# A fused causal convolution and gated MLP on one core: the first unit's convolution moved to channel-major taps, and the weights' first load cut in two

## The chip, the cores and the metric

The kernel runs on one core of a Trainium2 chip. Its time is the device time of one execution in microseconds (us). The core has a matrix engine (TensorE, PE in the profile, whose weight loads are shown as PEld), a vector engine (VectorE, DVE), a scalar engine with activation tables (ScalarE, ACT), a general engine (GpSimd, POOL) and a sync engine that only issues transfers and waits (SyncE, SP). "Line 552" or "L552" is a line of the kernel before.

## The reference

The input is `x` of shape 8 x 4096 x 192. Each of 8 heads (24 channels each) has 7 taps. The taps go through a softmax and then weight the last 7 positions, causally within each of the 8 sequences. The result, 32768 tokens of 192 channels, goes through a two-layer network with the activation h * cos(h):

```python
w = np.exp(weight - np.max(weight, axis=-1, keepdims=True))
w = w / (np.sum(w, axis=-1, keepdims=True) + 1e-09)          # 8 heads x 7 taps
out = np.einsum('hk,bskhg->bshg', w, x_unf)                   # causal, 7 taps
h = x @ w_in            # 192 -> 2048
g = h * np.cos(h)
return g @ w_out        # 2048 -> 192
```

## The kernel before, in words

**Tiling.** Tokens are worked on in 32 units of 1024, each of two tiles of 512 tokens, so there are 64 tiles. For a tile, the first product (`mm1`, L503) makes `h` in 8 pieces h0 to h7 of 256 hidden channels each: six matmuls per piece, in pairs that use the upper and the lower 64 rows of the array, into one buffer of a ring of three in PSUM (`h_pool`). ACT makes the cosine (`s0` to `s7`, L510), DVE multiplies (`g`, L514). The second product (`mm2_step`, L552) sums over the 16 blocks of hidden channels into two further PSUM banks (`o_pools`), in 64 steps of two matmuls per tile. Its results are copied to SBUF and stored.

**Convolution.** `mm1` wants the convolved tokens channel-major (`cT`). Units 4 to 31 use a path that the change does not touch. Units 1 to 3 cast x to bf16 on POOL (`cast_unit`, L219), multiply by a banded 128 x 128 matrix per head (`band`, L229), copy the token-major result to `ct`, double it and transpose it by a DMA. Unit 0 is the start of the kernel, and its path is written out by hand:

1. One small matmul (L150) spreads the 8 x 7 weights over the partitions. DVE and ACT do the softmax there (L176 to L185).
2. DVE multiplies a mask by the taps (`prod`, L401), sums over the taps (`diag`, L404), and 16 small copies spread the sums into `band`: seven on DVE, seven on POOL, two on ACT (L415).
3. The first half of x (4 blocks of 128 tokens) is cast on ACT (L219). 32 matmuls with `band` convolve it (`conv_first`, L432). The results are doubled on the way out (L438), turned by 12 matmuls against the identity (`turn_first`, L453) and copied into `cT` (L457).
4. The second half of unit 0 is loaded later, convolved behind h3 (`conv_rest`, code `r`, L465 and L472) and turned by a DMA transpose (code `X0`, L326).

**Order.** Nothing is scheduled automatically: each engine runs its instructions in the order in which the program writes them. For each tile a string gives PE's order and one gives ACT's. In these strings `h0` to `h7` are pieces of `mm1` (`h0a`, `h0b` are halves in tokens), `m11` is 11 steps of `mm2`, `w5` is five matmuls on zeros that only keep PE running (`keep_warm`, L136), `W0` and `W1` cast the two halves of `w_out` on POOL (L120), `K1` casts unit 1's x on POOL, `d11`, `c11` are the two halves of unit 1's banded convolution, `ed11`, `ed21`, `ec11`, `ec21` their copies on ACT, `D1` and `X1` its doubling and its transpose, `L2` loads unit 2. The ACT strings also set DVE's order, since each `s` is followed by its multiplication. For the first tile:

```python
PE_FIRST[0] = "K1 h0a h0b W0 h1 h2 h3 r h4 w5 d11 w4 h5 d21 W1 c11 X0 m1 h6 m11 h7 L2 c21 D1"
ACT_FIRST[0] = "s0a s0b s1 s2 er s3 s4 ed11 ed21 s5 ec11 s6 ec21 s7"
```

**Transfers.** `w_in` comes as two transfers on POOL's queue (`load_w`, L112), cast on the way. x and `w_out` come on SP's queue, in order. Two waits are put into that queue by hand: the second half of unit 0 and unit 1 wait for `diag`; `w_out` (L124) waits for the second copy of `conv_first`.

Of the kernel before, what the change touches and what calls it, by code (L numbers as in the profile page):

```python
# [16 lines left out]
def kernel(  # L17
# [14 lines left out]
    T = 512  # L32
# [25 lines left out]

    xf = x.rearrange("b s d -> (b s) d")
# [20 lines left out]
    w_row = consts.tile([4, HQ * K], FP32)  # L80
    nc.scalar.dma_start(out=w_row, in_=weight.rearrange("(q h) k -> q (h k)", q=4))
# [26 lines left out]
    w_src = moe_w_in.rearrange("(m k) (t f) -> t m k f", k=NC, t=2)  # L108
# [18 lines left out]

    one = consts.tile([128, 1], FP32)
    nc.vector.memset(one, 1.0)
    zero = consts.tile([128, T], BF16)  # L130
    nc.vector.memset(zero, 0.0)  # L131
    idle = o_pools[0].tile([128, T], FP32, name="o_ps0")

    def keep_warm(n, bank=idle):
        for _ in range(n):
# [3 lines left out]
    quarter = consts.tile([4, 128], FP32)  # L139
    nc.gpsimd.memset(quarter, 1.0)  # L140
    nc.gpsimd.affine_select(out=quarter, in_=quarter, compare_op=ALU.is_ge, fill=0.0, base=0, pattern=[[1, 128]],
                            channel_multiplier=-32)
    nc.gpsimd.affine_select(out=quarter, in_=quarter, compare_op=ALU.is_ge, fill=0.0, base=31, pattern=[[-1, 128]],
                            channel_multiplier=32)
# [4 lines left out]
    w_bc = w_all[:, 0 : HQ * K].rearrange("p (h k) -> p h k", k=K)  # L149
# [4 lines left out]
    xb0 = consts.tile([128, UB + 1, D], BF16, name="x_bf0")  # L154

    E = 32 + K - 1
    mask = consts.tile([128, E, K], BF16)
    nc.gpsimd.memset(mask[0:32], 0.0)
    nc.gpsimd.affine_select(out=mask[0:32], in_=mask[0:32], compare_op=ALU.not_equal, fill=1.0, base=1 - K,  # L159
                            pattern=[[1, E], [1, K]], channel_multiplier=-1)  # L160
    band = consts.tile([128, H, 256], BF16)
    nc.vector.memset(band, 0.0)
    for q, copy in enumerate((nc.vector.tensor_copy, nc.scalar.copy, nc.scalar.copy)):
        copy(out=mask[32 * q + 32 : 32 * q + 64], in_=mask[0:32])  # L164
    for t in range(2):
        load_w(t)
    nc.gpsimd.memset(xb0[:, 0, :], 0.0)
    ident = consts.tile([128, 128], BF16)
    nc.gpsimd.memset(ident, 0.0)
    nc.gpsimd.affine_select(out=ident, in_=ident, compare_op=ALU.not_equal, fill=1.0, base=0, pattern=[[1, 128]],  # L170
                            channel_multiplier=-1)
    wn = consts.tile([128, HQ, K], BF16)
    ct_bufs = [consts.tile([128, 2 * NC * NPB + 1, 64], BF16, name="ct_buf%d" % i) for i in range(2)]

    wmax = consts.tile([128, HQ, 1], FP32)
    nc.vector.tensor_reduce(out=wmax[:, :, 0], in_=w_bc, axis=mybir.AxisListType.X, op=ALU.max)  # L176
    wexp = consts.tile([128, HQ, K], FP32)
    nc.vector.tensor_tensor(out=wexp, in0=w_bc, in1=wmax.to_broadcast([128, HQ, K]), op=ALU.subtract)
    nc.scalar.activation(out=wexp, in_=wexp, func=AF.Exp)
    nc.scalar.activation(out=scrap, in_=one, func=AF.Sin)  # L180
    wsum = consts.tile([128, HQ, 1], FP32)
    nc.vector.tensor_reduce(out=wsum[:, :, 0], in_=wexp, axis=mybir.AxisListType.X, op=ALU.add)
    winv = consts.tile([128, HQ, 1], FP32)
    nc.vector.reciprocal(winv, wsum)
    nc.vector.tensor_tensor(out=wn, in0=wexp, in1=winv.to_broadcast([128, HQ, K]), op=ALU.mult)  # L185
    wo = consts.tile([128, NP, 2, D], BF16)

# [19 lines left out]
    def cast_unit(u, n0=0, n1=UB + 1, copy=nc.gpsimd.tensor_copy):  # L207
# [8 lines left out]
        if n0 == 0:  # L216
            bf[u] = xb0 if u == 0 else xbf_pool.tile([128, UB + 1, D], BF16, name="x_bf")
        o = 1 if u == 0 else 0
        copy(out=bf[u][:, n0 + o : n1 + o, :].rearrange("p n (h k r) -> p (n h) k r", k=NC, r=R),  # L219
# [3 lines left out]
    have = {("whole", 0, 0)}  # L223
# [24 lines left out]
    def conv_part(u, c, banks, whole=False):  # L248
# [6 lines left out]
        if u == 1 and c == 0:  # L255
            spread_taps(ps[1][:, nb * 2 * G : nb * 2 * G + K])
# [4 lines left out]
        for b in range(2):  # L261
            conv_out(u, c, ps, 0, 0, nb, nc.scalar.copy, banks=(b,))
            if b and u == 1 and c == 0:
                nc.scalar.copy(tap, ps[1][:, nb * 2 * G : nb * 2 * G + K])
            if b:
                have.add(("conv", u, c))
            yield
# [41 lines left out]
    def turn_unit(u, n0=0, n1=UB + 1, part=0):  # L309
# [12 lines left out]
        have.update((("turn", u), ("whole", u, 1)) if u == 0 else (("turn", u),))  # L322
# [9 lines left out]
    pick = consts.tile([128, 2, 2, 4, 2, R], BF16)  # L332

    def spread_taps(ps):

        for i in range(2):
            nc.tensor.matmul(out=ps, lhsT=pick[:, i].rearrange("p t q i r -> p (t q i r)"), rhs=wn[:, i, :],
                             start=i == 0, stop=i == 1, skip_group_check=True)

    rT, pa, ro = {}, {}, {}  # L340

    def turn_raw(u):
# [9 lines left out]
    def taps(u, j, half, mul):  # L352
        if u not in pa:
            pa[u] = pa_pool.tile([128, PA, WN, OR], FP32, name="pa")
# [371 lines left out]
```

## Time and profile before

| what | value |
|---|---|
| median of 3 runs | 705.23 us (705.06 to 705.26) |
| the profiled execution | 705.18 us, its span 703.5 us |
| PE busy | 697.0 us (99%) |
| DVE busy | 642.4 us (91%) |
| ACT busy | 644.4 us (92%) |
| POOL busy | 503.7 us (72%) |
| first `mm1` matmul (L503) | 10.60 us |
| first `mm2` matmul (L552) | 19.45 us |
| cast of `w_out`, first half / second half (L120) begins | 17.35 / 21.12 us |

Busy time is what the profile attributes to an engine's own instructions. Matmuls are pipelined and their ends are modelled, so PE's share says only that something was in it, not that it ran at its peak. The profile's clock column is the share of PE's clock that a throttle granted. In a timeline line the first number is the start in us, the second the time that the merged group covers; in brackets stands how long the engine had been idle before and what ended that. In the chain, each piece is what the next one waited for.

### The profile page before, as it was taken

Reading aid. Unit: us, or ns where it says so; the run is one execution under the profiler, and the core shown is the slowest. Engines: PE = TensorE matmul, PEld = TensorE weight load, DVE = VectorE, ACT = ScalarE, POOL = GpSimd, SP = SyncE. Lnnn points to the kernel's source line nnn. Section 1 sums busy time; section 2 is a strip of 40 time slices with the busy share of each in tenths; the row PEclk is TensorE's granted clock in tenths of the full one; section 3 lists DMA queues with packets and bytes.
Section 4 is the critical chain, followed back from the end, with each engine's and each line's share of the span. In section 5 each row is a group of like instructions: output and inputs, shape, how many; then the busy total and the mean of one; then the engine's idle time right before and its main releaser. Section 6 shows DMA issues by size and latency. Waiting matters only on the chain.

```text
span 703.5 us, 26826 instructions
## 1 busy us (share of the span) xinstructions
PE 697.0 (99%) x11830; PEld 512.8 (73%) x11830; DVE 642.4 (91%) x598; ACT 644.4 (92%) x831; POOL 503.7 (72%) x214
## 2 busy tenths in 40 slices
PE   8999999999999999999999999999999999999997
PEld 4677777777777777777777777777777777777776
DVE  6889999999999999999999999999999999999996
ACT  7889999999999999999999999999999999999875
POOL 6524478977778877778877688877789778799400
PEclk9999999999999999999999999999999999999999
DMA  8964456667667768676656577577665576874331
GB/s 214 234 167 97 120 135 143 138 147 164 138 153 146 131 145 176 134 152 131 147 152 153 150 159 129 140 161 150 143 147 132 145 174 137 153 127 95 92 91 47
DMA packets 228292, 100.09 MB, mean 142 GB/s; under 512 B 156240, under 2 KB 227792, under 8 KB 228176
## 3 DMA queue, kind: packets, MB, share of 16 engines
q1 hardware_dynamic: 227464, 97.40, 62.7%
q8 instruction: 92, 1.51, 0.9%
q0 software_dynamic: 416, 0.79, 0.7%
q14 instruction: 24, 0.20, 0.1%
q10 hardware_dynamic: 296, 0.20, 0.1%
HBM read 31.36 MB, written 25.17 MB: 80 GB/s over the span
## 4 chain that ended last, share of the span: by engine, by line
PE 96%; DMA 1%; DVE 1%; POOL 0%; SPq 0%; ACT 0%; issue 0%; POOLq 0%
PE o_ps L552 48%; PE h L503 46%; PE h L277 2%; DMA wo_f<-in_moe_w_out_dram 1%; PE h L552 0%; SPq L124 0%; PE h L229 0%; DVE band L415 0%; POOL wo L120 0%; POOL mask L159 0%; DVE ct L438 0%; PE o_ps L432 0%; ACT mask L164 0%; DVE diag L404 0%; DVE prod L401 0%
## 5 line engine op out<-in xcount | busy, mean ns | idle before, releaser
L514 DVE TENSOR_TENSOR g<-h,cs 128x1024 bf16<-128x1024 f32 (+1 forms) x513 | 604.9, 1216 | 27.9 <-ACT cs L510 24.5
L510 ACT ACTIVATE cs<-h 128x1024 bf16<-128x1024 f32 (+1 forms) x513 | 511.0, 1021 | 44.0 <-PE h L503 30.6
L552 PEld LDWEIGHTS <-g 64*128 64x128 bf16 x8192 | 354.2, 94 | 102.2 <-issue 1.0
L552 PE MATMUL o_ps<-wo,g 64*128 64x192 bf16 x8128 | 420.6, 243 | 0.1
L503 PE MATMUL h<-cT,w 64*128 64x512 bf16 (+1 forms) x3078 | 407.0, 376 | 0.8 <-DVE g L514 0.4
L503 PEld LDWEIGHTS <-w 64*128 64x128 bf16 x3078 | 147.6, 94 | 75.0 <-issue 1.8
L211 POOL CAST xk<-x_f 128x768 bf16<-128x768 f32 (+1 forms) x56 | 76.4, 1367 | 113.9 <-DMA x_f<-in_x_dram 109.3
L363 POOL TENSOR_TENSOR raw_prod<-rT,tap 128x2784 f32<-128x2784 bf16 x28 | 135.3, 4832 | 0.2
L370 POOL TENSOR_TENSOR raw_prod<-raw_prod,pa 128x2088 f32<-128x2088 f32 x28 | 129.1, 4609 | 2.2
L356 ACT ACTIVATE pa<-rT,tap 128x348 f32<-128x348 bf16 x168 | 94.6, 580 | 0.0
L374 POOL TENSOR_TENSOR raw_prod<-raw_prod 128x1392 f32<-128x1392 f32 x28 | 87.9, 3138 | 2.2
L571 DVE COPY o_sb<-o_ps 128x384 f32<-128x384 f32 x62 | 34.6, 557 | 23.7 <-PE o_ps L552 23.5
L377 POOL TENSOR_TENSOR ro<-raw_prod 128x696 bf16<-128x696 f32 x28 | 46.5, 1660 | 2.2
L294 ACT CAST ct_buf<-h 112x480 bf16<-112x480 f32 x56 | 28.6, 562 | 4.1 <-PE h L277 0.6
L571 ACT COPY o_sb<-o_ps 128x384 f32<-128x384 f32 x64 | 30.8, 482 | 0.1
L277 PE MATMUL h<-xk,band 64*112 64x120 bf16 x448 | 21.2, 213 | 0.0
L277 PEld LDWEIGHTS <-band 64*112 64x112 bf16 x448 | 18.0, 127 | 0.0
L219 POOL CAST x_bf<-x_f 128x768 bf16<-128x768 f32 (+2 forms) x5 | 9.1, 1812 | 7.0 <-DMA x_f<-in_x_dram 6.9
L307 POOL COPY ct<-ct 128x1728 bf16<-128x1728 bf16 x3 | 4.9, 1630 | 8.9 <-ACT ct L239 8.9
L394 POOL COPY cT<-cT 128x144 bf16<-128x144 bf16 x3 | 0.9, 308 | 13.5 <-DMA cT<-ct 13.5
L136 PE MATMUL o_ps<-zero 128*128 128x512 bf16 x21 | 7.2, 492 | 1.3 <-DVE zero L131 1.3
L239 ACT CAST ct<-h 128x432 bf16<-128x432 f32 x12 | 5.9, 530 | 0.4 <-issue 0.4
(66 smaller groups left out, 52.7 us busy)
## 6 DMA issues: line engine op xcount, KB each, us to landing
out_dram<-o_sb SPq DMA_DIRECT2D x63, 384.0 KB, 3.7
x_f<-in_x_dram SPq DMA_DIRECT2D x28, 480.0 KB, 5.5
x_f<-in_x_dram SPq DMA_DIRECT2D x56, 192.0 KB, 2.7
cT<-ro SPq DMA_DIRECT2D x112, 87.0 KB, 2.3
x_f<-in_x_dram SPq DMA_DIRECT2D x4, 384.0 KB, 5.6
wo_f<-in_moe_w_out_dram SPq DMA_DIRECT2D x4, 384.0 KB, 7.9
x_f<-in_x_dram SPq DMA_DIRECT2D x2, 768.0 KB, 5.2
cT<-ct_buf SPq DMA_TRANSPOSE x56, 4.0
```

The source lines that it names most:

```text
L211: copy(out=xk[u][:, NC * n0 : NC * n1].rearrange("p (k n) m -> p k n m", k=NC), in_=x_tiles[u][:, n0:n1].rearrange("p n (m k) -> p k n m", ...
L277: return nc.tensor.matmul(out=ps[h // 4][0:OP, 0 : NPB * 4 * G].rearrange("p (m i r) -> p i m r", m=NC * NPB, i=4)[:, h % 4], lhsT=band[si ...
L356: mul(pa[u][:, j, part], tap_window(u, j)[:, part], tap[:, j : j + 1])
L363: nc.gpsimd.tensor_tensor(out=p, in0=tap_window(u, PA, K), in1=tap[:, PA:K].rearrange("p (j a b) -> p j a b", a=1, b=1).to_broadcast([128, ...
L370: add(out=p[:, 0:m], in0=p[:, 0:m], in1=a[:, done : done + m], op=ALU.add)
L374: add(out=p[:, 0:m], in0=p[:, 0:m], in1=p[:, n - m : n], op=ALU.add)
L377: add(out=ro[u], in0=p[:, 0], in1=p[:, 1], op=ALU.add)
L503: nc.tensor.matmul(out=h[:, i, n0 * 128 : n1 * 128], lhsT=w[rows, k, j, :], rhs=rhs, start=(k == 0), stop=(k == NC - 1))
L510: nc.scalar.activation(out=cs[:, :, part], in_=h[:, :, part], func=AF.Sin, bias=math.pi / 2.0, scale=1.0)
L514: nc.vector.tensor_tensor(out=g_tiles[t][:, 2 * j : 2 * j + 2, part], in0=h[:, :, part], in1=cs[:, :, part], op=ALU.mult)
L552: ms.append(nc.tensor.matmul(out=o_ps[tt, b, si], lhsT=g_tiles[tt][rows, f, s * 128 : (s + 1) * 128], rhs=wo[rows, f // 2, f % 2, :], star ...
L571: (copy or copies[b])(o_sb[t][:, 2 * b : 2 * b + 2, :].rearrange("p s d -> p (s d)"), o_ps.pop((t, b)))
```

## The change

All of it is in the start of the kernel. From the second tile on the order of every engine is the same as before, apart from numbers of buffers.

- **Taps.** The weights stay one head per row (8 x 7), and a matrix `head` of -1 spreads them so that partition p holds the taps of the head of channel p. The softmax is one minimum, one exponential with the sum taken along by ACT, one reciprocal and one product. `double` and the taps give `diag`: 7 diagonal matrices (`make_diag`, two DVE products).
- **Unit 0.** x comes in three transfers that are issued at once (blocks 0-1, 2-3, 4-7). Each pair of blocks is cast by itself (`cast_first`: ACT, ACT, POOL, ACT), turned first, by six matmuls against the identity (`turn_pair`), copied to `xT`, and then convolved channel-major by 14 matmuls, 7 taps for each block of the pair (`conv_pair`), straight into `cT`'s layout. Pairs 0 and 1 come before `h0a`, pair 1 turned behind pair 0; pairs 2 and 3 are turned there too and convolved as `v2` and `v3` in the first tile's string; their copies are shared between ACT and DVE. `conv_first`, `turn_first`, `conv_rest` and the DMA transpose `X0` are gone.
- **`band`** for units 1 to 3 is made from `wide`, `wb` and `prod`, `bands`. All 16 copies into `band` are on POOL.
- **`w_in`** comes in four transfers, two per column half. The first two are issued early on POOL, the second two behind POOL's cast of blocks 4-5. Pieces h0 to h3 use the first half, h4 to h7 the second.
- **SP's queue.** One wait by hand is left: unit 1's x, and `w_out` behind it, wait for the copy of pair 0's second block.
- **Fillers.** Of 24 matmuls on zeros (3, 9, 2, 1, 5, 4) six are left (3, 2, 1).

```diff
-    nc.scalar.dma_start(out=w_row, in_=weight.rearrange("(q h) k -> q (h k)", q=4))
+    nc.scalar.dma_start(out=w_row, in_=weight)
-    def load_w(t):
-        nc.gpsimd.dma_start(out=w[64 * t : 64 * t + 64].rearrange("p k j f -> p k (j f)"), in_=w_src[t])
-    load_unit(0, 0, NB)
+    def load_w(t, a):
+        nc.gpsimd.dma_start(out=w[64 * t : 64 * t + 64, :, a * HP : (a + 1) * HP].rearrange("p k j f -> p k (j f)"), in_=w_src[t, a])
+    load_unit(0, 0, NB // 2)
+    load_unit(0, NB // 2, NB)
+    load_unit(0, NB, UB)
...
+    for t in range(2):
+        load_w(t, 0)
     keep_warm(3)
-    nc.tensor.matmul(out=w_all[:, 0 : HQ * K], lhsT=quarter, rhs=w_row, start=True, stop=True)
-    keep_warm(9)
+    nc.tensor.matmul(out=w_bc, lhsT=head, rhs=w_row, start=True, stop=True)
+    keep_warm(WARM[0])
+    nc.vector.tensor_reduce(out=wmax, in_=w_bc, axis=mybir.AxisListType.X, op=ALU.min)
+    nc.scalar.activation(out=wexp, in_=w_bc, func=AF.Exp, bias=wmax, scale=-1.0, accum_out=wsum)
...
+    def turn_pair(p, ps):
+        to = ps[:, 0 : NC * (EDGE + 128)].rearrange("p (k t) -> p k t", k=NC)
+        for k in range(NC):
+            for prev, t0, t1 in ((0, EDGE, EDGE + 128), (1, 0, EDGE)):
+                n = 2 * p + 1 - prev
+                nc.tensor.matmul(out=to[:, k, t0:t1], lhsT=xb0[:, k, n : n + 2, :].rearrange("p n m -> p (n m)"),
+                                 rhs=ident[:, 128 - (t1 - t0) : 128], start=True, stop=True, skip_group_check=True)
+        return to
+    def conv_pair(p, ps, j0=0, j1=K):
+        for j in range(j0, j1):
+            for i in range(2):
+                rows = slice(64 * i, 64 * i + 64)
+                nc.tensor.matmul(out=ps[i][:, 0 : NC * 128].rearrange("p (k t) -> p k t", k=NC),
+                                 lhsT=diag[rows, j].rearrange("p t m -> p (t m)"), rhs=xT[rows, p, :, j : j + 128],
+                                 start=j == 0, stop=j == K - 1, skip_group_check=True)
...
+    cast_first(0, 2, nc.scalar.copy)
+    to = [turn_pair(0, ring_banks()[0])]
+    keep_warm(WARM[1])
+    cast_first(2, 4, nc.scalar.copy)
+    to.append(turn_pair(1, ring_banks()[0]))
+    make_diag(0, 4)
+    nc.vector.tensor_copy(out=xT[:, 0], in_=to[0])
+    nc.scalar.activation(out=scrap, in_=one, func=AF.Sin)
+    cast_first(4, 6, nc.gpsimd.tensor_copy)
+    for t in range(2):
+        load_w(t, 1)
+    nc.scalar.copy(out=xT[:, 1], in_=to[1])
+    cast_first(6, 8, nc.scalar.copy)
+    make_diag(4, K)
+    ps0 = conv_pair(0, [o_bank(0), ring_banks()[0]])
+    conv_copy(0, 0, ps0, copies[0])
+    m = conv_copy(0, 1, ps0, copies[1])
+    to = [turn_pair(2 + i, rest[i]) for i in range(2)]
+    nc.scalar.copy(out=xT[:, 2:4], in_=bass.AP(to[0].tensor, to[0].offset, [to[0].ap[0], [T, 2], [1, NC * (EDGE + 128)]]))
+    ps1 = conv_pair(1, [ring_banks()[0], o_bank(1)])
+    nc.vector.tensor_reduce(out=bands, in_=prod, axis=mybir.AxisListType.X, op=ALU.add)
+    nc.gpsimd.tensor_copy(out=tap, in_=wn)
+    conv_copy(1, 0, ps1, copies[0])
+    conv_copy(1, 1, ps1, copies[1])
+    tc.add_manual_dep(nc.sync.nop().ins, m.ins.name, sync_dep, reason="order of the transfers")
     load_unit(1, 0, NB)
     load_unit(1, NB, UB)
     load_edges(1)
+    load_wo(0)
+    load_wo(1)
+    for i in range(16):
+        q, rows = divmod(i, 4)
+        nc.gpsimd.tensor_copy(out=band[32 * rows : 32 * rows + 32, HQ * q : HQ * (q + 1), 32 * rows : 32 * rows + E],
+                              in_=bands[32 * q : 32 * q + 32])
...
-    PE_FIRST = ["K1 h0a h0b W0 h1 h2 h3 r h4 w5 d11 w4 h5 d21 W1 c11 X0 m1 h6 m11 h7 L2 c21 D1",
+    PE_FIRST = ["K1 h0a h0b h1 v2 h2 h3 v3 W0 h4 d11 h5 d21 W1 c11 m1 h6 m11 h7 L2 c21 D1",
-    ACT_FIRST = ["s0a s0b s1 s2 er s3 s4 ed11 ed21 s5 ec11 s6 ec21 s7",
+    ACT_FIRST = ["s0a s0b s1 ev2 ev2 s2 s3 ev3 ev3 s4 ed11 ed21 s5 ec11 s6 ec21 s7",
```

More of the change, by code (lines that the diff above doesn't have):

```diff
@@ L161 @@
[L161 to L171, printed above, removed]
@@ L321, in turn_unit @@
         assert ("double", u) in have
[L322 removed]
+        have.add(("turn", u))
         ct = ct_tiles.pop(u)
@@ L360, in conv_raw @@
     def conv_raw(u):
+        assert {("tap", u, j, half) for j in range(PA) for half in range(2)} <= have
         a, p = pa.pop(u), raw_prod
```

224 lines of the change are left out of this document (91 added, 133 removed), and 13 rows, old and new, of tables (ACT_FIRST, PE_FIRST).

## The prediction, on record before the changed kernel was run

> **What bounds the kernel now.** I read the page's engine table and its chain first. PE is busy for 697.0 of 703.5 us and makes 96% of the chain that ended last, so the end moves only if PE's list gets shorter or PE starts its unbroken work at another time.
>
> ```profile
> PE 697.0 (99%) x11830; PEld 512.8 (73%) x11830; DVE 642.4 (91%) x598; ACT 644.4 (92%) x831; POOL 503.7 (72%) x214
> PE 96%; DMA 1%; DVE 1%; POOL 0%; SPq 0%; ACT 0%; issue 0%; POOLq 0%
> ```
>
> From the second tile on, the change leaves every engine's order as it is. So next I asked for the chain in order of time over the first 60 us. Columns: start, length, what.
>
> ```profile
> 8.90 0.97 DVE ct L438
> ...
> 12.16 8.84 DMA wo_f<-in_moe_w_out_dram
> 21.00 0.02 issue
> ...
> 21.12 1.48 POOL wo L120
> ...
> 22.64 0.34 PE o_ps L552 x4
> ```
>
> The chain runs from the first convolution's second copy to the fourth transfer of `w_out`, its cast (W1) and `mm2` step 16 at 22.64 us. Behind that there is only PE. The question is by how much step 16, and the DVE products beside it, come sooner. The timeline shows what else stands close (start, length, engine; idle time before in brackets):
>
> ```profile
> 5.34 0.15 PEld L136 LDWEIGHTS <-zero 128*128 128x128 bf16 x1 [0.28 <-issue]
> 5.77 0.15 PEld L136 LDWEIGHTS <-zero 128*128 128x128 bf16 x1 [0.28 <-issue]
> 6.12 0.10 PEld L136 LDWEIGHTS <-zero 128*128 128x128 bf16 x1 [0.20 <-issue]
> 6.13 2.00 POOL L415 CAST band<-diag 32x76 bf16<-32x76 f32 x7 [0.73 <-DVE diag L404]
> 10.60 1.62 PE L503 MATMUL h<-cT,w 64*128 64x256 bf16 x18 [0.18 <-DVE cT L457]
> 13.77 2.81 POOL L219 CAST x_bf<-x_f 128x768 bf16<-128x768 f32 x2
> 16.62 0.53 PE L229 MATMUL h<-x_bf,band 128*128 128x216 bf16 x4
> 17.05 1.02 PE L136 MATMUL o_ps<-zero 128*128 128x512 bf16 x4
> 18.21 0.82 PE L503 MATMUL h<-cT,w 64*128 64x512 bf16 x6
> 21.41 0.82 PE L503 MATMUL h<-cT,w 64*128 64x512 bf16 x6 [0.15 <-DVE g L514]
> 25.87 5.96 DVE L514 TENSOR_TENSOR g<-h,cs 128x1024 bf16<-128x1024 f32 x5
> 29.69 0.30 PEld L229 LDWEIGHTS <-band 128*128 128x128 bf16 x4 [0.16 <-DVE g L514]
> ```
>
> Three readings. d11 (16.62) follows POOL's two casts of unit 1 (13.77 to 16.58). h7 (21.41) waits for DVE to free a ring buffer. In the second tile DVE runs without a gap, and at 29.69 a weight load waits for it: PE has hardly any slack over DVE there. So bringing W1 forward alone buys little: the gain is the smaller of PE's and DVE's.
>
> **The change, part by part.** Clock times are from the span's start. From engine to engine I add the 0.02 to 0.05 us of the chain's "issue" pieces.
>
> *Taps.* Removed: the mask (POOL 0.97, ACT 0.83), a subtraction and a reduction (0.17 each). DVE's new memset of `head` stands ahead of `zero`, which PE waits for: 128 elements at the `band` memset's 0.91 us per 1024 are some 0.15 us, so PE starts at 1.45 instead of 1.31. Three fillers at 0.427 (the step from 5.34 to 5.77) and the tap matmul (0.60) end at 3.37. Reduction 0.17, exponential 0.21 plus an unknown for the sum (0 to 0.2, between no cost and a second such instruction; I take 0.05, as no operand is larger), reciprocal 0.17, product 0.17: `wn` at 4.25, against 4.73.
>
> *First two pairs.* Before, 393 KB of x landed 3.4 us after its issue; half of it lands no later than 4.2 us and, by the 1.6 us for which it was seen moving, near 3.5. An ACT cast of half the columns costs between 0.6 (half of L219's 1.21) and 1.21 if it were all fixed; with 384-column copies at 0.48 beside it I take 0.7. The casts then end at 4.57 and 5.3. A turn is six matmuls, three of them six columns wide: between 0.34 (six full turns of L453) and 1.0 (six steps of weight load 0.15 at the slower pace). I take 0.9 for the first, as the slow pace still holds there, and 0.45 for the second: 5.5, a filler, 6.4. DVE's copy of the first (0.58, from 0.56 for 384 columns) ends at 6.23, and `diag` was made before that (0.48, as `prod`). `conv_pair` is seven pairs of 384 columns. L503 takes 0.65 on the chain for three pairs of 512, so 0.163 a pair, 1.14 in all and 0.15 for the last one's drain: 6.45 to 7.75. No row shows this matmul itself; without overlap of the two row halves it would be 2.3.
>
> *Bands.* DVE's copy of pair 0 (0.56) ends at 8.36, `bands` (0.72, L404's form) at 9.12. Then 16 copies on POOL alone. Seven took 2.00, so 16 take 4.6 (3.9 by their busy time; I take the pace, since they stand in the same row). They end at 13.7, and the two casts of unit 1 (2.81) at 16.55. That is where it was, 16.58: what the taps win, nine more copies on POOL take back. Both x transfers of unit 1 now follow pair 0's copy (8.4): at 5.6 to landing 14.0, 15.2 for the second, which is just under the time when POOL asks. Behind SP's wait for that copy stand unit 1's x, `w_out` and unit 2's x, in this order; unit 0's second half no longer does.
>
> *h0a.* ACT's table load (1.28) and the scrap (0.20) now stand behind the second cast: 6.8. Copy of turn 1 (0.5), last cast (0.7): 8.08. The last turns end at 8.65, `conv_pair` 1 at 9.85, its copies at 10.45. h0a starts at 9.9 against 10.60, and g0a at 11.1 against 11.77.
>
> *Inside the first tile.* Nine fillers (1.25 and 1.02) and `conv_rest` (0.85; ACT 1.50) go. `v2` and `v3` cost PE 1.15 each, ACT 0.48 each, DVE 0.56 each. DVE: g1 12.75, copy, g2 14.55, g3 15.75, copy, g4 17.55. PE: d11 at 16.6; h5 right behind it at 17.2 instead of 18.21. But ACT has s4 until 17.5 and the two copies of d11 until 18.5, so s5 starts at 18.5 (before 19.07) and g5 at 19.55 (20.13). h7 waits for g5: 21.0 (21.41). s7 21.8, g7 22.85 (23.32). DVE is 0.47 sooner.
>
> *w_out.* The DMA transpose X0 (issued at 16.00, 3.92 us of SP) goes, and `w_out` has to move behind unit 1's x from about 13.4 at the 340 GB/s of the 10 to 18 us rows: 1.57 MB, 18.0. POOL casts W0 16.6 to 18.1 and W1 to 19.6 (before 22.6). Step 16 then waits for nothing but the list: h7 at 21.0, 0.65, four steps 0.33: 22.0, against 22.64. PE is 0.64 sooner.
>
> *w_in.* The first half is issued near 3.0 as before with half the bytes; the second behind POOL's cast of blocks 4-5 (6.0), two issues of 0.72, landing at 7.4 plus at most 6.6: 14.0. h4 asks at 15.8. Cover 1.8 us; were it gone, each us late moves h4 by one.
>
> *Sum.* PE 0.64 and DVE 0.47 sooner; DVE leads and PE has about 0.1 of slack: minus 0.5 us on an execution of 705.18 (span 703.5 and 1.68 around it): 704.7. The median is 0.05 above that execution, so the same figure stands. With all lower bounds (turns 0.34, casts 0.6, copies 3.9) the tile starts 0.8 sooner still, 703.9; with the upper ones (casts 1.0, turns 1.0, sum 0.2) 0.9 later than forecast and more, 705.9.
>
> **A rule against the change.** In the rows, filler matmuls come every 0.43 us until 5.77, then 0.35, and later five take 1.25: PE doubles its pace at about 6.04, although the clock column reads 1.00 in every stretch. From 3.24 to 6.72 PE was then filled with nine fillers; now it has two there, a tap matmul, two small ones, a turn and one filler, with gaps waiting for ACT. The Trainium skill, "TensorE: Matmul & The Clock Gate", Part 1, says that the array runs at half rate until one free-running window of about 3.4 us was busy. By that rule a window not counted as busy keeps the half rate until about 9.45. By the rows alone: the pace could stay slow, and that is the third rival.
>
> **The rivals.**
>
> - *DVE runs through.* If d11 comes by 15.5 (copies and casts on POOL quicker) and nothing makes ACT late, DVE has only its own work from 11.1: 1.3 for the halves, seven products of 1.2, two copies: g7 ends at 21.9 instead of 24.55, and PE is 2.1 sooner, being held by h7 and W1 (19.6 and on). 703.1. For it: DVE was the last wait in this stretch. Against: the walk shows three gaps by ACT's order.
> - *The slow pace lasts to about 9.5.* `conv_pair` 0 takes 1.15 more, so `bands` 10.3, d11 17.8, and h0a 11.0: 1.1 behind the forecast, 705.8. For it: seven of nine fillers gone. Against: PE still has work for some 85% of that stretch.
> - *Slower: the slow pace lasts through the first tile.* Each us of it past 6.4 costs PE 0.5 us on the path; it ends above 706.6 once it lasts past some 10.3. To 12.9 it costs 3.2 against the forecast, 707.9. For it: PE waits for ACT twice between 6.4 and 9.9. Against: three matmul groups fill most of that.
>
> **How the numbers follow.** Forecast 0.52, within 0.2% (1.41 us, about what a measurement of this kernel can tell from no change). DVE runs through 0.23, faster by more. Slow to 9.5: 0.13, within. Slow through: 0.12, slower. The forecast's own bounds of 703.9 to 705.9 lie within 0.2%. Of the forecast's 0.52 I leave 0.02 to faster and 0.03 to slower, for the bounds' far ends. Faster 0.25, same 0.60, slower 0.15. The range reaches down to the first rival, 703.1, and up to the point from which the last decides, 706.6.
>
> **What would show it.** h0a near 9.9, d11 near 16.6, g5 near 19.5, step 16 near 22.0, and no wait for W1. DVE's waits between 11 and 23 us tell the first rival; the spacing of the 384-column matmuls (0.16 or 0.32 a pair) tells the others. Wrong it would be if the two row halves did not overlap, or if a transfer that I call covered is last: `w_in`'s second half at h4, unit 1's x at POOL's casts.

## The result, and the profile after

The changed kernel took 705.97 us (median; 705.62 to 709.12) against 705.15 us (705.04 to 705.32) before: a ratio of 1.0016, with a 95% interval of 1.0010 to 1.0023. It is 0.82 us slower. The forecast was 704.7, half a microsecond faster; the time lies inside the range and inside the 0.2% called "the same", but the change is real and has the other sign. The profiled execution took 706.02 us, its span 704.2 (before 705.18 and 703.5). Over all executions the median span is 704.2 against 703.4, and the time around the span 1.80 against 1.70: some 0.1 of the 0.82 lies outside what the trace shows. Three executions of the changed kernel, at 707.5 to 709.1 us, had a mean granted clock of 0.997 to 0.998 where all the others had 0.999 to 1.000; what such a clock means here is shown under the experiments.

The chain of the changed kernel in order of time (start, length, what):

```profile
8.01 0.32 PE o_ps L419
...
8.39 0.57 DVE cT L426
...
8.98 0.37 SPq L103
...
10.79 0.41 SPq L127
...
11.24 7.93 DMA wo_f<-in_moe_w_out_dram
...
19.23 1.48 POOL wo L123
...
20.75 0.26 PE o_ps L553 x2
...
23.21 0.49 PE o_ps L553 x12
23.71 0.65 PE h L504 x6
```

Before, the chain went over the *second* half of `w_out` (W1 at 21.12) to step 16 at 22.64. Now it goes over the *first* half: W0 starts at 19.23 (before 17.35), and the first `mm2` step stands at 20.75 (before 19.45). Behind it PE has only its list: 12 steps, h6, h7, four more steps of the group at 23.21 (0.33 us, as forecast), so step 16 is at 23.54. A cleaner mark is the piece of `mm1` behind that group: 23.71 against 22.98 before, 0.73 later. The span grew by 0.7. So the whole loss is made before 24 us, and the steps to look at are those that lead to 20.75. The timeline (start, length, engine; in brackets idle time before and what ended it):

```profile
3.82 1.30 ACT L397 CAST x_bf<-x_f 128x384 bf16<-128x384 f32 x2
...
5.91 0.50 PE L419 MATMUL o_ps<-xT,diag 64*128 64x384 bf16 x1
...
9.63 4.52 POOL L481 CAST band<-bands 32x76 bf16<-32x76 f32 x16 [1.35 <-DVE bands L468]
9.77 0.38 PE L419 MATMUL h<-xT,diag 64*128 64x384 bf16 x1
...
9.99 0.32 PE L419 MATMUL h<-xT,diag 64*128 64x384 bf16 x1
10.65 0.49 PE L504 MATMUL h<-cT,w 64*128 64x256 bf16 x6
...
17.36 0.54 PE L229 MATMUL h<-x_bf,band 128*128 128x216 bf16 x4
17.94 0.82 PE L504 MATMUL h<-cT,w 64*128 64x512 bf16 x6
...
20.75 0.26 PE L553 MATMUL o_ps<-wo,g 64*128 64x192 bf16 x2 [0.85 <-POOL wo L123]
```

The taps came as forecast; both casts end at 5.12 instead of 5.3 and both turns at 5.97 instead of 6.4, so `conv_pair` 0 began at 5.91 instead of 6.45. But its pairs follow each other at 0.32 us (the first line of the chain is one of them), not 0.163; the spacing halves only between 9.77 and 9.99. So it ends at 8.37 instead of 7.75, and DVE's copy, on which SP's wait for unit 1's x and `w_out` stands, ends at 8.95 instead of 8.36. And PE waits 0.85 us for W0, where the forecast had `w_out`'s cast well ahead. The stretches of 1 us (busy time of PE, PEld, DVE, ACT and POOL with counts; granted clock; share of the 16 DMA engines; GB/s), first before, then after:

```profile
8.00:9.00 1.00, 0.97 (x26) 0.66 (x24) 0.10 (x1) 0.50 (x1) 0.13 (x1) 1.00 0.95 160
9.00:10.00 1.00, 0.94 (x11) 0.48 (x10) 0.96 (x2) 0.57 (x2) 0.00 (x0) 1.00 1.08 242
10.00:11.00 1.00, 0.82 (x13) 0.50 (x12) 0.99 (x2) 0.69 (x2) 0.00 (x0) 1.00 1.09 369
```
```profile
9.00:10.00 1.00, 1.00 (x12) 0.50 (x12) 0.57 (x1) 0.74 (x1) 0.33 (x2) 1.00 1.03 156
10.00:11.00 1.00, 1.00 (x16) 0.56 (x12) 0.12 (x1) 0.25 (x2) 0.85 (x4) 1.00 1.09 152
11.00:12.00 1.00, 0.64 (x12) 0.41 (x10) 0.58 (x2) 0.82 (x2) 0.83 (x5) 1.00 0.92 213
12.00:13.00 1.00, 1.00 (x14) 0.52 (x12) 0.88 (x2) 0.92 (x2) 0.87 (x4) 1.00 1.04 332
```

In both kernels the DMA engines are full in these rows (a share near 1). What differs is what fills them. The low figures, 150 to 160 GB/s, belong to `w_in`, which is cast on the way (786 KB are written, twice that is read); 330 to 370 belongs to x and `w_out`. In slices of 0.6 us the step to above 250 GB/s comes at 9.6 before and at 11.4 after, 1.8 us later. W0 starts 1.88 us later (19.23 against 17.35), but these two figures are not one delay. Before, 0.39 MB of unit 0's x still move behind that step; after, they have moved ahead of it.

The trace also keeps the 16 updates of a semaphore by which each of these transfers tells its landing; the landing counts when the last has come. For the second transfer of `w_out`'s first half, 15 of the 16 came by 17.73 (before 17.00), and the last at 19.18 (before 17.23). So most of the transfer is 0.7 us late, and one lagging update makes up the rest. An estimate from these figures: without the lag the cast would have begun at 17.78 and ended at 19.26, ahead of d21's end at 19.90, and PE would not have waited for it. In both profiles one packet of 16 KB moves near by, on the queue that the profile calls `instruction`: from 15.87 to 17.00 after, from 17.00 to 18.11 before, where it is the next transfer whose last update lags (15 by 18.23, the last at 19.90). In nine of the sixteen profiles of this case the first transfer of x or `w_out` to land behind that packet has such a lag, of 0.8 to 1.8 us. That the packet causes it is not shown.

### The profile page after: what moved, and what is told of

Same layout as the page of the kernel before. It is cut to its first block, busy times and chain, and to the rows that moved or that the text cites. A ratio compares the mean times of both kernels' runs of the same rounds, so it can differ in the third digit from the quotient of the medians.

```text
span 704.2 us, 26828 instructions
## 1 busy us (share of the span) xinstructions
PE 697.0 (99%) x11832; PEld 531.5 (75%) x11832; DVE 642.5 (91%) x597; ACT 643.8 (91%) x830; POOL 505.0 (72%) x222
## 4 chain that ended last, share of the span: by engine, by line
PE 97%; DMA 1%; SPq 0%; DVE 0%; POOL 0%; issue 0%; ACT 0%
PE o_ps L553 48%; PE h L504 47%; PE h L273 2%; DMA wo_f<-in_moe_w_out_dram 1%; PE h L553 0%; PE o_ps L419 0%; PE o_ps L152 0%; PE h L229 0%; POOL wo L123 0%; SPq L103 0%; PE h L411 0%; SPq L88 0%; DVE cT L426 0%; PE o_ps L172 0%; SPq L127 0%
## 5 line engine op out<-in xcount | busy, mean ns | idle before, releaser
L553 PEld LDWEIGHTS <-g 64*128 64x128 bf16 x8192 | 365.5, 94 | 92.3 <-issue 1.5
L553 PE MATMUL o_ps<-wo,g 64*128 64x192 bf16 x8128 | 426.3, 243 | 0.8 <-POOL wo L123 0.8
L504 PE MATMUL h<-cT,w 64*128 64x512 bf16 (+1 forms) x3078 | 412.3, 376 | 0.4 <-DVE cT L426 0.4
L504 PEld LDWEIGHTS <-w 64*128 64x128 bf16 x3078 | 160.5, 94 | 66.6 <-DVE cT L426 0.6
L219 POOL CAST x_bf<-x_f 128x1728 bf16<-128x1728 f32 (+2 forms) x4 | 7.8, 1966 | 0.1
L419 PE MATMUL o_ps<-xT,diag 64*128 64x384 bf16 x42 | 7.0, 366 | 0.2 <-DVE cT L426 0.2
```

The costliest lines, as they stand in the source:

```text
L504: nc.tensor.matmul(out=h[:, i, n0 * 128 : n1 * 128], lhsT=w[rows, k, j, :], rhs=rhs, start=(k == 0), stop=(k == NC - 1))
L553: ms.append(nc.tensor.matmul(out=o_ps[tt, b, si], lhsT=g_tiles[tt][rows, f, s * 128 : (s + 1) * 128], rhs=wo[rows, f // 2, f % 2, :], star ...
```

## The experiments

Two disputed causes came out of these rows: the half pace of PE up to 9.8 us ("pace"), and the first half of `w_out` that lands late ("w_out"). They are chained, since SP lets x and `w_out` go only behind a copy that the slow `conv_pair` 0 delays. A short table first; the difference is to the kernel before as measured beside it, the columns behind it are from the profiled execution. "15 of 16" is the time by which 15 of the 16 updates of the first half of `w_out` had come (17.00 before); W0 is its cast. The mark is the start of the `mm1` piece behind step 17 in the chain, 22.98 before (for x2_late, whose chain does not pass there, the timeline of both kernels is used). Its delay and the span's should agree where nothing later stalls; it is left out where the list or the pace puts another piece there.

| run | median, us | difference | 15 of 16 | W0 | mark - 22.98 | span - 703.5 |
|---|---|---|---|---|---|---|
| changed kernel | 705.97 | +0.82 | 17.73 | 19.23 | +0.73 | +0.7 |
| x2_late | 706.90 | +1.78 | 18.64 | 19.47 | +0.96 | +2.1 |
| six_fillers | 706.55 | +1.43 | 18.24 | 18.61 | +0.10 | +0.1 |
| before, few_fillers | 706.36 | +1.24 | 16.90 | 17.11 | +1.12 | +1.2 |
| before, no_w5_w4 | 705.68 | +0.56 | 16.96 | 17.12 | +0.98 | +1.0 |
| w_whole | 708.15 | +3.06 | 17.65 | 17.77 | | +1.7 |
| m1_behind_h6 | 705.98 | +0.89 | 18.00 | 19.89 | | +1.4 |
| w_whole_six_fillers | 709.12 | +4.03 | 18.17 | 18.50 | | +4.4 |
| release_early | 705.09 | 0.00 | 18.26 | 18.51 | +0.05 | +0.2 |
| release_fillers | 708.00 | +2.86 | 19.51 | 19.68 | +2.45 | +2.5 |
| two_releases | 705.18 | +0.04 | 17.16 | 18.08 | -0.42 | -0.4 |
| before, wo_early | 705.11 | -0.03 | 17.01 | 17.27 | | 0.0 |
| two_releases_fillers | 707.26 | +2.13 | 19.22 | 19.95 | +2.28 | +2.3 |
| x1_at_diag | 705.13 | -0.02 | 17.92 | 18.62 | +0.12 | +0.2 |
| x1_at_diag_fillers | 705.43 | +0.28 | 16.54 | 17.04 | -0.47 | -0.5 |

**Is it unit 2's x?** In the changed kernel it is asked for at 14.02 instead of 20.02, because the DMA transpose no longer holds SP's queue, and it moves beside `w_out`. This run holds it behind W1.

```diff
+                if v == 2:
+                    tc.add_manual_dep(nc.sync.nop().ins, wo_casts[1].ins.name, sync_dep, reason="order of the transfers")
```

> The changed kernel, with unit 2's x held in SP's queue until the second half of w_out has been cast. Theory A (w_out is late because unit 2's x, issued at 14.0 us in the changed kernel's profile and at 20.0 us before, shares the DMA engines with it): the first half of w_out lands by about 17.8 us instead of 19.2, its cast ends by 19.3, mm2's first step waits for c11 alone (19.9 instead of 20.75), 705.1 to 705.3 us. Theory B (the slow pace of PE through pair 0 alone sets the tile, and w_out's landing is covered by it): no change, 705.9 to 706.0 us.

Measured: 706.90 us, ratio 1.0026 [1.0017, 1.0036]. W0 did not come sooner (19.47). By itself that does not settle the question, since in this execution all of the stream ran later (`w_in`'s last part landed at 13.00 instead of 12.10). But the two transfers of the first half came 1.19 us apart, by 15 of their 16 updates, against 1.16 in the changed kernel. So unit 2's x took nothing from them there. The extra microsecond is another one: x of unit 2 is now really late, and PE waits for it at 31.79. From the timeline of this run:

```profile
19.47 1.47 POOL L125 CAST wo<-wo_f 128x1536 bf16<-128x1536 f32 x1 [1.63 <-DMA wo_f<-in_moe_w_out_dram]
...
29.20 2.54 POOL L221 CAST x_bf<-x_f 128x1728 bf16<-128x1728 f32 x1 [4.14 <-DMA x_f<-in_x_dram]
31.79 0.53 PE L231 MATMUL h<-x_bf,band 128*128 128x216 bf16 x4 [1.07 <-POOL x_bf L221]
```

**Is the pace a matter of fillers?** Six fillers behind the tap matmul instead of two:

```diff
-    WARM, OUT = (2, 1), ((0, 1), (0, 1))
+    WARM, OUT = (6, 1), ((0, 1), (0, 1))
```

> The changed kernel with six fillers instead of two behind the tap matmul, four more of 0.427 us. Theory C (PE's pace doubles when a stretch of about 3.4 us was filled with dense matmuls): the pace doubles near 6.0 us as before the change, pair 0's taps come every 0.16 us instead of 0.32, so that pair 0 ends near 8.4 us in spite of a start 1.5 us later, and what follows is 0.2 to 0.4 us sooner: 705.5 to 706.0 us. Theory D (the moment depends on something else): pair 0 keeps 0.32 us a tap and ends 1.5 us later: 707.2 to 707.5 us.

The other way round, on the kernel before, two fillers instead of nine ahead of the first convolution:

```diff
-    keep_warm(9)
+    keep_warm(2)
```

> The kernel before with two fillers instead of nine behind the tap matmul. Theory C: the 32 matmuls of the first convolution and the 12 turns run at the slow pace, the pace doubles only past 9 us, the first products start 0.7 to 1.5 us later than 10.60 us, and the time is 705.5 to 706.5 us. Theory D: the pace still doubles near 6.0 us and the time stays at 705.1 to 705.2 us.

Both say yes. With six, the pairs come every 0.16 us from the first (7.22, 7.39, 7.56 and on), W0 starts 0.6 us sooner and the profiled span is 703.6. With two in the kernel before, the half pace lasts to about 11.5, the first `mm1` comes at 11.65 instead of 10.60, and the kernel takes 706.36 us, ratio 1.0017 [1.0007, 1.0026]. From the timelines, first six_fillers, then few_fillers:

```profile
7.22 0.33 PE L419 MATMUL o_ps<-xT,diag 64*128 64x384 bf16 x1 [0.21 <-DVE xT L449]
7.39 0.32 PE L419 MATMUL o_ps<-xT,diag 64*128 64x384 bf16 x1
```
```profile
8.99 1.03 PE L136 MATMUL h<-zero 128*128 128x512 bf16 x2
9.81 0.85 PE L453 MATMUL h<-ident,ct 128*128 128x128 bf16 x6
```

But the median of six_fillers is no better: 706.55 us (705.57 to 709.65), ratio 1.0025 [1.0014, 1.0036]. The profiled execution was its best. Its median span is 704.2, that of the changed kernel, so nothing is gained. But this prices two things together: the fillers start the first convolution 1.3 us later (7.22 against 5.91), so that DVE's copy of pair 0 ends at 9.18, no sooner than the 8.95 of the changed kernel, and SP is let go no sooner. And its time around the span was 1.74 to 3.34 us, where the changed kernel has 1.73 to 1.83.

**Do the nine fillers around d11 hold h5 back?** The forecast took 1.0 us for them. Undone alone, on the kernel before:

```diff
-    PE_FIRST = ["K1 h0a h0b W0 h1 h2 h3 r h4 w5 d11 w4 h5 d21 W1 c11 X0 m1 h6 m11 h7 L2 c21 D1",
+    PE_FIRST = ["K1 h0a h0b W0 h1 h2 h3 r h4 d11 h5 d21 W1 c11 X0 m1 h6 m11 h7 L2 c21 D1",
```

> The kernel before without the nine fillers around d11. The prediction's step (the fillers held h5 back by 1.0 us): h5 starts near 17.2 us instead of 18.21, the products g5 to g7 come 0.4 to 0.6 us sooner, but the second half of w_out still lands at 21.0 us, so that mm2's step 16 stays at 22.6 us: 705.0 to 705.2 us. If the landing did not bind: 704.5 us. If the fillers kept the pace up: 705.5 us and more, with matmuls at half pace behind d11.

Measured: 705.68 us, ratio 1.0008 [0.9999, 1.0017], in two groups: five executions at 705.0 to 705.2, five at 706.1 to 706.3 with a mean clock of 0.997 to 0.998. The profiled one is of the second group. Its timeline:

```profile
16.67 0.53 PE L229 MATMUL h<-x_bf,band 128*128 128x216 bf16 x4 [1.09 <-POOL x_bf L219]
18.25 1.46 PE L503 MATMUL h<-cT,w 64*128 64x512 bf16 x6 [1.02 <-DVE g L514]
```

h5 started at 18.25, as with the fillers (18.21): it waits for DVE's product to free its buffer. The fillers stood in idle time and cost nothing. What they did is seen in the 1.46 us of h5, which is 0.82 before. Without them PE is busy for 0.33 and 0.23 us in the two stretches before 18, and then runs at half pace; the clock column says so here (0.59, 0.50, 0.50, 0.71 from 18 to 22 us).

**Is it the second halves of `w_in`?** Both transfers whole again, at the first place:

```diff
-    def load_w(t, a):
-        nc.gpsimd.dma_start(out=w[64 * t : 64 * t + 64, :, a * HP : (a + 1) * HP].rearrange("p k j f -> p k (j f)"), in_=w_src[t, a])
+    def load_w(t):
+        nc.gpsimd.dma_start(out=w[64 * t : 64 * t + 64].rearrange("p k j f -> p k (j f)"), in_=w_src[t])
...
-        load_w(t, 0)
+        load_w(t)
...
-    for t in range(2):
-        load_w(t, 1)
```

> The changed kernel with w_in in two whole transfers again, both issued where the first halves were. Theory E (the second halves, issued at 6.8 us behind POOL's cast, keep the DMA engines at 120 to 170 GB/s until 11.9 us instead of 10.0, and unit 1's x and w_out wait behind that): the engines reach 300 GB/s near 10.5 us, the first half of w_out lands by 17.8 us instead of 19.2, mm2's first step waits for c11 only (19.9 instead of 20.75), 705.1 to 705.3 us. Theory F (the landing is set by the moment at which SP may issue, 10.8 us, after pair 0's copy): landing at 19.0 to 19.2 as now, 705.8 to 706.0 us.

```profile
10.76 0.28 PE L502 MATMUL h<-cT,w 64*128 64x256 bf16 x1 [0.59 <-DMA w<-in_moe_w_in_dram]
12.85 1.47 PE L502 MATMUL h<-cT,w 64*128 64x256 bf16 x17 [1.81 <-DMA w<-in_moe_w_in_dram]
...
17.77 1.47 POOL L123 CAST wo<-wo_f 128x1536 bf16<-128x1536 f32 x1 [0.76 <-DMA wo_f<-in_moe_w_out_dram]
```

W0 came at 17.77, 1.5 us sooner than in the changed kernel, with SP's issues at the same moments. But 15 of the 16 updates had come by 17.65, as in the changed kernel (17.73); what this execution lacks is the lag of the last (17.72 against 19.18). So it does not show that the place of `w_in`'s second halves holds `w_out` back. And the kernel takes 708.15 us, ratio 1.0041 [1.0028, 1.0053], since the first products now wait 0.59 and 1.81 us for `w_in`: in the changed order unit 0's second half goes ahead of it. The split pays for itself here. With six fillers on top of it (the two diffs above together):

> Both: w_in whole and early, and six fillers behind the tap matmul. If the slow pace and w_in's second halves are the two causes, h0a starts near 10.2 us, the first half of w_out lands near 17.3 us, and the time comes to the forecast's 704.6 to 704.9 us in the executions in which the pace does not fall again; theory F gives 705.5 us.

709.12 us, ratio 1.0055 [1.0040, 1.0071]. PE waits for `w_in` again, and its pace falls to half once more (granted clock 0.50 from 13 to 19 us). Fillers ahead of a stretch in which PE must wait anyway do not last through it.

**Does a sooner h6 help?** The first `mm2` step moved behind h6, so that ACT and DVE get h6 a microsecond earlier:

```diff
-    PE_FIRST = ["K1 h0a h0b h1 v2 h2 h3 v3 W0 h4 d11 h5 d21 W1 c11 m1 h6 m11 h7 L2 c21 D1",
+    PE_FIRST = ["K1 h0a h0b h1 v2 h2 h3 v3 W0 h4 d11 h5 d21 W1 c11 h6 m12 h7 L2 c21 D1",
```

> The changed kernel with the first step of mm2 behind h6 instead of ahead of it, so that h6 no longer queues behind the wait for w_out's cast; the landing is untouched. Theory G (the cost of the late w_out is that h6, and with it ACT's and DVE's next piece, stands behind the waiting step): h6 starts at 19.9 us instead of 20.83, g6 and g7 come 0.5 to 0.9 us sooner, 705.2 to 705.5 us. If PE's own backlog of mm2 were what counts: 705.8 to 706.0 us.

705.98 us, ratio 1.0015 [1.0006, 1.0025]: nothing gained. h6 went from 20.83 to 19.82, but `mm2` began at 21.41, again behind W0. So in this stretch a sooner h6 is worth nothing while `w_out` is late; its W0 was late by the same kind of lag (15 of the 16 updates by 18.00, the last at 19.84).

**Let the transfers go earlier.** SP's wait tied to DVE's copy of the first turn (ends 5.8 us) instead of pair 0's copy (8.95), called release_early:

```diff
-    nc.vector.tensor_copy(out=xT[:, 0], in_=to[0])
+    turned = nc.vector.tensor_copy(out=xT[:, 0], in_=to[0])
...
-    tc.add_manual_dep(nc.sync.nop().ins, m.ins.name, sync_dep, reason="order of the transfers")
+    tc.add_manual_dep(nc.sync.nop().ins, turned.ins.name, sync_dep, reason="order of the transfers")
```

> The changed kernel with SP's wait tied to DVE's copy of the first turn (5.8 us) instead of the copy of pair 0's second block (8.95 us): unit 1's x and w_out may be issued 3.2 us sooner. Theory F: w_out lands 2 to 3 us sooner (16.5 us) and the time is 705.1 us. Theory E: the engines are as full as before between 7 and 12 us, x and w_in share them, w_out lands at most 0.5 to 1 us sooner, 705.4 to 705.8 us, with w_in's second half later at h4.

705.09 us, ratio 1.0000 [0.9991, 1.0009]: the whole loss of 0.82 us is gone. W0 came at 18.51 instead of 19.23. The issue of `w_out` moved by 3.2 us, its landing by 0.7, and 15 of the 16 updates came no sooner than in the changed kernel (18.26 against 17.73). So the loss is gone in the median, but this profile does not show `w_out` as a whole coming sooner; what is shorter in it is the lag of the last update, 0.2 us. Unit 1's x now shared the DMA engines with `w_out` and its second part came late (d11 at 17.97). With x released at 5.8 as there, and `w_out` by a second wait, at pair 0's copy (two_releases; the diff is on top of the last one):

```diff
+    tc.add_manual_dep(nc.sync.nop().ins, m.ins.name, sync_dep, reason="order of the transfers")
     load_wo(0)
```

> Unit 1's x released by the copy of the first turn (5.8 us) as in e8, but w_out held until pair 0's copy (8.95 us) as in the changed kernel. If what counts is that the DMA engines are free for these transfers and not when SP may issue them: w_out's first half lands 0.3 to 0.7 us ahead of the changed kernel's 19.2 us, unit 1's x no longer waits behind w_out (d11 at 17.4 us instead of e8's 18.0), 705.0 to 705.4 us. If w_out's own issue time counts: landing at 19.2 us and 705.8 us.

705.18 us, ratio 1.0001 [0.9992, 1.0010]. The chain of this run goes the same way as that of the changed kernel, without the issues of x; `conv_pair` 0 is just as slow in it (0.32 us a pair), and yet W0 comes 1.15 us sooner. (In the profiles of release_early and of this run the pace doubled near 9 us, before the second tap of pair 1. That alone brings no gain: in x2_late it had doubled by then too.) The chain:

```profile
8.40 0.57 DVE cT L426
...
8.98 0.38 SPq L127
...
9.40 8.63 DMA wo_f<-in_moe_w_out_dram
...
18.08 1.48 POOL wo L123
...
19.60 0.26 PE o_ps L554 x2
...
22.56 0.65 PE h L505 x6
```

The same kind of freedom in the kernel before, without its second wait (`w_out` asked for at 8.53 instead of 9.89):

```diff
-        tc.add_manual_dep(nc.sync.nop().ins, m.ins.name, sync_dep, reason="order of the transfers")
         load_wo(0)
```

> The kernel before without its second wait in SP's queue: w_out is issued right behind unit 1's x, near 8.6 us instead of 9.9. The prediction's reading of the kernel before (mm2's step 16 waits for w_out's fourth transfer): it lands 0.3 to 1.2 us sooner than 21.0 us, step 16 comes by 22.0 to 22.4 us, 704.6 to 705.0 us. If the DMA engines are full and only share the same bytes differently: landing at 21.0 us, unit 1's x later, 705.1 to 705.5 us.

705.11 us, ratio 0.9999 [0.9990, 1.0008]; W0 17.27, W1 21.08. There the landing did not follow the moment of the issue.

**Pace on top of the release.** If half pace is a cost of its own, six fillers should now bring it in. Once on release_early, once on two_releases (the diff is that of six_fillers):

> The early release of e8 with six fillers behind the tap matmul. It prices the slow pace with SP's queue uncoupled from pair 0's copy. If the slow pace costs time only by holding back SP's queue: no gain over e8's 705.09 us, or a loss where the pace falls again in the gap ahead of mm2. If it also costs by the late products: h0a near 9.9 us, mm2's step 16 0.3 to 0.5 us ahead of e8's 22.7 us, 704.6 to 704.8 us.

> The changed kernel with the release of unit 1's x tied to the first turn's copy, of w_out to pair 0's copy (as two_releases), and six fillers instead of two behind the tap matmul. Theory pace (the half pace of the first convolution is a cost of its own, beside w_out's lateness, which the two releases take away): conv_pair 0 at 0.16 us a pair ends near 8.4 though it starts near 7.2, first products 0.3 to 0.4 sooner, d11 near 16.9 or earlier, W0 near 18.0, and a median 0.2 to 0.4 below that of two_releases: 704.8 to 705.0. Theory w_out (the start is bound by the transfers, and an earlier first product only waits longer): W0 near 18.1 as in two_releases, PE idle for 0.5 us or more ahead of it, the pace falling to half behind the idle stretch, and a median of 705.2 to 706.5.

They lost: 708.00 us, ratio 1.0036 [1.0022, 1.0050], and 707.26 us, ratio 1.0027 [1.0018, 1.0036]. In the second run the pairs come at 0.16 us from 6.91 on, but x of unit 1 lands at 17.60, PE stands idle and its pace falls. Its chain, its stretches (PE busy and count, granted clock, DMA share, GB/s) and two lines of its timeline:

```profile
7.29 10.31 DMA x_f<-in_x_dram
...
17.66 1.47 POOL x_bf L219
...
19.17 0.88 PE h L229 x4
```
```profile
17.00:18.00 1.00, 0.60 (x5) 1.00 1.10 332
18.00:19.00 1.00, 0.00 (x0) 1.00 1.02 301
19.00:20.00 1.00, 0.83 (x6) 0.52 0.97 295
20.00:21.00 1.00, 1.00 (x7) 0.50 1.10 353
```
```profile
6.46 1.25 POOL L113 DMA_DIRECT2D w<-in_moe_w_in_dram  x2
6.88 0.92 SPq L103 DMA_DIRECT2D x_f<-in_x_dram  x2
```

The last two lines tell why. The fillers hold the first turn back and with it SP's release, so unit 1's x is asked for at 6.88, behind `w_in`'s second halves (6.46); in two_releases it was 5.79, ahead of theirs (6.74). So these two runs do not test the pace. The next pair does: x is let go by DVE's first diagonal product, which no PE work precedes, once with two fillers and once with six.

```diff
-        nc.vector.tensor_tensor(
+        return nc.vector.tensor_tensor(
...
-    make_diag(0, 4)
+    made = make_diag(0, 4)
...
-    tc.add_manual_dep(nc.sync.nop().ins, turned.ins.name, sync_dep, reason="order of the transfers")
+    tc.add_manual_dep(nc.sync.nop().ins, made.ins.name, sync_dep, reason="order of the transfers")
```

> As two_releases, but unit 1's x is let go by DVE's first diagonal product (ends near 5.05) instead of the first turn's copy (5.8), so that no PE work stands ahead of it; w_out at pair 0's copy as there; two fillers. Both theories: x of unit 1 is asked for at 5.1, ahead of w_in's second halves (6.7), d11 near 16.9, W0 near 18.0, and a median within 0.3 of two_releases: 704.9 to 705.4. It is the partner of x1_at_diag_fillers.

> As x1_at_diag, with six fillers instead of two. The fillers no longer hold back unit 1's x, which in two_releases_fillers was asked for at 6.88, behind w_in's second halves at 6.46. Theory order (what decides is whether x is asked for ahead of w_in's second halves): x lands in time, d11 by 17.0, W0 near 18.0, no stretch at granted clock 0.5, and a median within 0.3 of x1_at_diag, 704.9 to 705.4, since the pace has no cost of its own. Theory pace (the half pace costs something by itself once the transfers are in order): 0.3 to 0.5 below x1_at_diag: 704.5 to 704.8. Theory idle (an earlier first product only makes PE wait longer and its pace fall): 706.0 to 707.5, with the clock at 0.5 behind 18 us, as in two_releases_fillers.

705.13 us, ratio 1.0000 [0.9991, 1.0009], and 705.43 us, ratio 1.0005 [0.9996, 1.0014]. The median spans are 703.3 and 703.4: with the transfers asked for in time, the fillers are worth nothing on balance, since the surer pace comes with a later start of the convolution (7.27 against 5.91). The pace with two fillers varies: in the profiled execution of x1_at_diag it opened at about 6.6 by itself. DVE's copy of pair 0 then ended at 8.25, and `w_out` was asked for at 8.27. Yet W0 came at 18.62, later than the 18.08 of two_releases at half pace, and the first products waited 0.91 us for `w_in`. With six fillers x was asked for at 5.16, ahead of `w_in` at 6.94, and there is no fall of the pace; so the late request of x was the cause of the two losses above. That its place behind `w_in` is what made it late is not shown: the changed kernel asks for x at 8.98, behind `w_in` too, and has it by 15.36, sooner than the 17.60 above. What remains of the difference between the medians lies around the span (1.74 to 3.35 us with six fillers, 1.73 to 1.85 with two). In the profiled execution with six fillers W0 even came at 17.04, and yet `mm2` starts no sooner than in the kernel before (19.45). Its chain:

```profile
15.15 2.35 DVE g L516 x2
17.51 0.47 DVE cT L426
...
18.01 0.95 ACT ct L239 x2
...
19.00 0.53 PE h L229 x4
19.53 0.19 PE o_ps L554 x2
```

With `w_out` in time the next thing in the way is the order on DVE and ACT ahead of d21 (19.00). In this execution the mark is 0.47 sooner and the span 703.0. None of the variants is faster than the kernel before; release_early, two_releases and x1_at_diag are level with it.

## Why the prediction was wrong

- **The step that failed: "w_out has to move behind unit 1's x from about 13.4 at the 340 GB/s", and with it "Step 16 then waits for nothing but the list".** By that sum the first half of `w_out` has moved by 15.7 and W0 can start at 16.6. Measured: W0 at 19.23, the first `mm2` step held for 0.85 us, step 16 at 23.54 instead of 22.0. Unit 1's x itself landed as forecast (15.36 against 15.2), so the lateness is that of `w_out`: 15 of 16 updates by 17.73, the last at 19.18. The forecast gave the first half neither a margin for its landing nor a wait. That the transfers behind SP's wait make the loss is shown: with them released earlier, and nothing else changed, the 0.82 us are gone (release_early, two_releases, x1_at_diag). By which way the release does it stays open. That `w_in`'s second halves, which keep the rate low until nearly 12 us, are what delays `w_out` is argued and not shown (w_whole), and so is the `instruction` packet. The cover that was given for h4 held.
- **The step ahead of it: "PE doubles its pace at about 6.04".** It stayed at half until 9.77 to 9.99. The start of `conv_pair` 0 was 0.54 us better than forecast, its end 0.62 worse, and SP's release with it. That fillers make the early doubling sure is seen in both kernels; x1_at_diag had it near 6.6 with two. The rule cited there (the Trainium skill, "TensorE: Matmul & The Clock Gate", Part 1) was the better guide in this execution: it gave about 9.45. The second rival, "the slow pace lasts to about 9.5", had 705.8 and is 0.2 us off, but partly by luck: its path was d11 at 17.8 and h0a at 11.0, and they came at 17.36 and 10.65, while the end was set by `w_out`, which it did not name. As a cost of its own the pace was not found in the changed kernel: made sure by fillers, with a later start, it left the median span where it was, alone or with the transfers asked for in time. What it costs without the later start was not priced by any pair of medians. (The two slow rivals also do not agree with each other: at the third's 0.5 us for each us past 6.4, a slow pace to 9.5 gives 706.2, not 705.8.) In the kernel before, where the pace was lost further (to 11.5 us), it cost 1.2 us.
- **"h5 right behind it at 17.2 instead of 18.21"** counted 1.0 us for the nine fillers. The run without them shows that they had held nothing back; they had kept PE's pace. In the changed kernel h5 came at 17.94, as both d11 (17.36 and on) and DVE's product (to 17.88) were through.
- **"DVE leads and PE has about 0.1 of slack"** was the wrong bound as long as `w_out` is late: with h6 a microsecond earlier nothing was gained, and the span follows the mark behind step 17 to 0.2 us in every run without a later stall.
- **What was right:** that only the first tile decides, the taps, the overlap of the two row halves (0.32 us a pair at half pace, 0.16 at full), the 16 copies on POOL (4.52 against 4.6 forecast), that W1 would no longer be waited for, and that PE's 0.33 us from the mark's group to step 16 stays. The kernel slower than before by more than 0.2%, the last rival, did not come: the slow pace ended at 9.9, below its 10.3.

The gain of 0.5 that was forecast is seen in the span of single executions alone: two_releases and x1_at_diag_fillers had 703.1 and 703.0 in their profiled ones (the second still took 706.35 us, with 3.35 around its span). On the median span it stays at 0.0 to 0.1. What makes the difference from run to run is left open, as is what fills the time around the span with six fillers.

## What to carry to other kernels

A transfer has not landed when its bytes would have moved at the full rate: it counts when its last part is told, and one part alone can be late. So give the transfer whose reader stands on the path a margin, and read a late landing by its parts before a change of rate elsewhere is blamed for it. Here the forecast had the data by 15.7, most of it came by 17.73 and the last part at 19.18. Before an instruction is made the trigger of a queue of transfers, ask how late it may get if its engine is at half pace. Fillers in idle time can be what keeps an engine's pace, so cost their removal by what runs behind them, not by their own length.

## What the runs showed of the hardware

- PE was busy for 0.82 to 1.00 of every microsecond from 2 to 10 us, mostly in matmuls of 7 or 128 columns and in 64-row pairs, and yet stayed at half pace until 9.8. With the same instructions on PE up to there the pace doubled between 8.3 and 9.1 in two_releases, release_early, w_whole and x2_late, and near 6.6 in x1_at_diag. With nine or six fillers of 512 columns it doubled near 6.0. The Trainium skill, "TensorE: Matmul & The Clock Gate", Part 1, says that the window is free-running and that the moment varies from run to run; the rows agree with the varying. It counts a window by whether it was busy, and no row here tells what "busy" takes.
- The granted clock reads 1.00 in this first stretch at half pace, but 0.50 where the pace falls again later. It fell after idle stretches of 1.0 to 1.6 us with little work around them: PE busy for 0.33 and 0.23 us in two stretches of 1 us (no_w5_w4), 0.60 and none in the two ahead of 19 us (two_releases_fillers). The same page's section "Why this matters for your kernels" advises against gaps above some 3 us; here shorter ones were enough. They do not always do it: in w_whole PE was busy for 0.04 and 0.15 us in the two stretches from 11 to 13 us, in x2_late for 0.11 from 17 to 18 and 0.01 from 20 to 21, and the granted clock stayed at 1.00. In no_w5_w4 and two_releases_fillers the fall lasted about 3 us and shows as a mean clock of 0.997 (about 6 us and 0.995 in w_whole_six_fillers). A mean of 0.997 to 0.998 is also what the three long executions of the changed kernel had; that they had the same cause is argued, not shown.
- The 16 updates by which a transfer tells its landing do not come together. Between the 15th and the last lay 0.0 to 1.9 us for the transfers of `w_out`: 0.04 and 1.45 us for the first two in the changed kernel, 0.05 and 0.07 in w_whole, 0.25 and 1.84 in m1_behind_h6.
